# First inverse DFT of a spectral layer as unsplit fp32 products on 32x64 tiles of TensorE, read straight from the second layer's output

## The chip, the core and the metric

One core of a Trainium2 chip runs the whole kernel: TensorE (PE), with its own queue of weight loads (PEld), VectorE (DVE), ScalarE (ACT), GpSimd (POOL), and SyncE (SP), which mostly issues DMAs. The metric is the device time of one execution in microseconds, as the median of several runs; the kernel before takes 1437.01 us (three runs, 1436.25 to 1438.35).

## The reference

The input is 4096 rows of 640 values. It runs through a layer norm, a spectral layer, a residual, a second layer norm and a SwiGLU feed-forward layer (width 1728). The change is inside the spectral layer:

```python
Xf = rfft2(x)                                  # 2049 wave numbers x 640
z  = Xf.reshape(B, H, Wf, NB, BS)              # 4 blocks of 160 columns
h  = relu(complex matmul of z with w1, + b1)   # first layer, per block
o  = complex matmul of h with w2, + b2         # second layer, per block
o  = sign(o) * max(abs(o) - 0.01, 0)           # soft threshold, real and imaginary part
y  = irfft2(o)
```

## The kernel before, in words

**The transforms.** 4096 is 128 x 32, so each DFT is made of two: the forward one of products with 128x128 constants (`dft_a`, then `stage_b`), the inverse one of a first inverse DFT over 32 wave numbers each (`stage_i`) and a second one over 64 complex rows (`first_y` for the first rows, the feed-forward layer's row chains for the rest). The result of the first inverse DFT goes to the DRAM tensor `s2`, from which the second one reads it.

**Chunks and blocks.** The spectrum is cut into 8 chunks `ch` (256 wave numbers each; chunk `CE` = 4 has two more), and each chunk into 4 blocks `b` of 160 columns. A hand-written loop runs over `p = 4*ch + b` from 0 to 31 and writes out the order of the instructions of every engine (`manual_schedule`); `LAST` is 28, and p = 29 to 31 and what follows have code of their own, which I call the tail. In a step p of the loop, TensorE does in this order: the first layer of block p (`stage_l1`, tile `pl`, 21 products of 256 columns), the second forward DFT of a later block (`stage_b`, tile `pb`; two of them where b is 1), the second layer of block p - 1 (`stage_l2`, tile `pc`, 16 products of 320 columns), and the first inverse DFT of row block p - 7 (`stage_i`, tile `pi`).

**From the second layer to the first inverse DFT.** `stage_l2` adds the bias on VectorE and writes the tile `tt` (two per chunk, `q` = 0, 1; 128 wave numbers as rows, real and imaginary parts side by side, 640 columns). A row block i of a chunk needs 64 of these wave numbers, real parts in rows 0 to 63 and imaginary parts in rows 64 to 127; so `move_x` copies them with two DMAs on SP's queue into a tile `xx` (56 DMAs in all). Then ScalarE makes the two halves of the soft threshold (`shrink_parts`), VectorE subtracts them (`shrink`), ScalarE rounds the result to `xh` (`shrink_high`), VectorE takes the rest `xl` (`shrink_low`): operands in the format fp32r are kept as a rounded high part and a low part. `stage_i` makes three fp32r products per half of 320 columns (xh with the constant's high part, xl with it, xh with its low part), six per row block; ScalarE copies each half to a tile `co`, and POOL issues its DMA to `s2`. Chunks 0 to 6 make 28 such row blocks.

**The last chunk** does without the moves: `inverse_last` takes `tt` directly, 64 of its rows at a time, in plain fp32, the real and the imaginary part as two products of 320 columns into the same tile. In the trace each fp32 product stands as two records. Half 0 of its columns runs behind `stage_l2` of the last block, half 1 behind the products `py` of `first_y`, which begin the second inverse DFT of the first four rows. After these come the transposes `pt` and the first products `pg` of the feed-forward layer.

**PSUM.** There are eight banks: tags `p1`, `p2`, `p3` with two each, and `b0`, `b1`. `pl` takes both p1 and, as its third tile, one p3; `pc` takes p2; `pi` takes p3, one bank per half. The third tile of `pl` comes free when ScalarE has copied `u0` out of it and VectorE has made `u1` from it (line 764). A group of products waits for the engine that last read its bank, and what stands behind it in TensorE's queue waits with it.

Of the kernel before, what the change touches and what calls it, by code (L numbers as in the profile page):

```python
# [13 lines left out]
P = 128  # L14
# [32 lines left out]
def constants():  # L47
# [63 lines left out]
    bm = bm.reshape(2, 128, 128)  # L111
    bi = bm[1].reshape(2, 64, 128)

    bx = np.tile(bm[1].reshape(2, 64, 128).transpose(1, 0, 2), (2, 1, 1)).reshape(128, 256)
    bmh, bml = _hl(bm)
    bm = np.stack([bmh, bml], axis=1)
    bm = np.ascontiguousarray(bm.transpose(2, 0, 1, 3)).reshape(128, 2 * 2 * 128)
# [12 lines left out]
    for n in range(4):  # L130
        for h in range(2):
            for r in range(2):
                for i in range(2):
                    m = 4 * (4 * ORDER[-1] + 2 * h + i)
                    ge[64 * i:64 * i + 64, n, 256 * h + 128 * r:256 * h + 128 * r + 128] = (
                        bi[r].reshape(64, 4, 32)[:, :, n] @ ga[n, m:m + 4])
        ge[:, n, 512:] = ga[n]
# [9 lines left out]
        "k_bm": f(bm),  # L147
# [24 lines left out]
def body(tc, x, w1, b1, w2, b2, wg, wu, wd, c, wm, k_fa, k_tb, k_tx, k_bm, k_bx, k_ga, k_ge, k_id, out, dbg=None):  # L172
# [29 lines left out]
    with ExitStack() as top:  # L202
# [34 lines left out]
        with ExitStack() as af:  # L237
# [4 lines left out]
            bm = wp.tile([P, 2, 2, 128], F32R, name="bm")  # L242
# [289 lines left out]
            bx = p2.tile([P, 2, 128], F32, name="bx")  # L532
# [9 lines left out]
            nc.sync.dma_start(bx.rearrange("p a b -> p (a b)"), k_bx)  # L542
# [86 lines left out]
            def stage_b(ch, t):  # L629
                g, tb = gs[ch], tbs[ch]  # L630
                tag = {(0, 1): "p2", (1, 1): "p3"}.get((ch, t))
                pb = (ps.tile([P, 2, 256], F32, tag=tag, name=f"pb{ch}_{t}") if tag else
                      bank0(1 if t == 4 else 0, [P, 2, 256], f"pb{ch}_{t}"))
                col = slice(128 * t, 128 * t + 128)
                for j in range(4):
                    mm(pb[:, :, 64 * j:64 * j + 64], g[:, j, col], tb[:, j, :], start=True, stop=True)
                pbs[ch, t] = pb
# [140 lines left out]
            def stage_l2(ch, b, then=()):  # L778
                h0, h1, r2, _ = hss[ch, b]
                late = []  # L780
                de = slice(160 * b, 160 * b + 160)
                for q in range(3 if ch == CE else 2):
# [3 lines left out]
                    if b == 0 and q < 2:  # L786
                        tts[ch, q] = p2.tile([P, 2, D], F32, tag="tt", bufs=2, name=f"tt{ch}_{q}")
# [13 lines left out]
                    if q < 2:  # L801
                        dve.tensor_tensor(tts[ch, q][:, :, de], pc[:, :320].rearrange("p (r e) -> p r e", r=2),
# [3 lines left out]
                    else:  # L806

                        dve.tensor_tensor(tts[ch, 0][0:1, 1, de], pc[0:1, :160], b2t[0:1, 0, b, :], op=OP.add)
                for q, (pc, seq) in enumerate(late):
                    for i, (l, m) in enumerate(seq):  # L810
                        mm(pc[:, :320], l, m, start=False, stop=(i == 2))
                    dve.tensor_tensor(tts[ch, q][:, :, de], pc[:, :320].rearrange("p (r e) -> p r e", r=2),
                                      b2t[:, :, b, :], op=OP.add)

            xxs = {}

            def move_x(ch, i):
                q, h = i // 2, i % 2
                xx = p2.tile([P, D], F32, tag="xx", bufs=5, name=f"xx{ch}_{i}")
                for r in range(2):  # L820
                    nc.sync.dma_start(xx[64 * r:64 * r + 64, :], tts[ch, q][64 * h:64 * h + 64, r, :])
                xxs[ch, i] = xx


            def shrink_parts(ch, i):
                xx = xxs[ch, i]
                act.activation(cl, xx, AF.Relu, bias=nlam)
                act.activation(xx, xx, AF.Relu, bias=nlam, scale=-1.0)

            def shrink(ch, i):  # L830
                xx = xxs[ch, i]
                if 4 * ch + i < LAST - 5:
                    dve.tensor_tensor(xx, cl, xx, op=OP.subtract)
                else:
                    dve.tensor_scalar(cl, xx, LAM, -LAM, op0=OP.min, op1=OP.max)
                    dve.tensor_tensor(xx, xx, cl, op=OP.subtract)

            def shrink_high(ch, i):
                xx = xxs[ch, i]
                xh = p2.tile([P, D], F32R, tag="xh", bufs=2, name=f"xh{ch}_{i}")  # L840
                xl = p2.tile([P, D], F32R, tag="xl", bufs=2, name=f"xl{ch}_{i}")
                act.activation(xh, xx, AF.Copy)
                xxs[ch, i] = (xh, xl, xx)

            def shrink_low(ch, i):
                xh, xl, xx = xxs[ch, i]
                dve.tensor_tensor(xl, xx, f32(xh), op=OP.subtract)

            def stage_i(ch, i):
                J = 4 * ORDER[ch] + i  # L850
                kd = 0 if J == 0 else 1
                xh, xl, _ = xxs[ch, i]
                co = p2.tile([P, D], F32, tag="co", bufs=2, name=f"co{J}")
                for hf in range(2):
                    e = slice(320 * hf, 320 * hf + 320)
                    pi = (bank0(0, [P, 512], f"pi{J}_{hf}") if ch == NCH - 2 and i % 2 and hf == 0 else
                          ps.tile([P, 512], F32, tag="p3", name=f"pi{J}_{hf}"))
                    mm(pi[:, :320], bm[:, kd, 0, :], xh[:, e], start=True, stop=False)
                    mm(pi[:, :320], bm[:, kd, 0, :], xl[:, e], start=False, stop=False)
# [1705 lines left out]
```

## Time and profile before

| what | value |
|---|---|
| median of three runs | 1437.01 us (1436.25 to 1438.35) |
| profiled execution, first to last instruction | 1434.9 us |
| granted TensorE clock | 1.000 |
| TensorE busy | 1401.5 us (98%) |
| VectorE, ScalarE, POOL busy | 1097.0, 783.8, 538.0 us |
| products of `stage_i` (lines 858 to 860) | 56 of each line, 108.3 to 288.3 us from the start |
| products of `inverse_last` (line 906) | 32 records, 288.7 to 311.1 us |
| `move_x` (line 821) | 56 DMAs of 160 KB |

The spectral layer's loop fills the stretch from about 90 to 262 us, its tail that up to 314 us; the feed-forward layer takes the rest. In the views, `pi<-xh,bm` is a group of instructions that writes tile `pi` from `xh` and `bm`, xN is how many there are, and L858 is a line of the kernel. A record's duration on PE includes the time in which it drains while the next one runs; how long a product holds the engine is seen from start to start.

### The profile page before, as it was taken

The numbers are of one execution on the slowest core, as the hardware profiler recorded it, in microseconds if no ns is written. First come the engines' busy times: TensorE is split into PE (matmuls) and PEld (weight loads), VectorE is DVE, ScalarE is ACT, GpSimd is POOL, SyncE is SP. The second block draws the span as 40 slices with busy tenths as digits, with TensorE's granted clock in tenths as the row PEclk, the third lists the DMA queues.
The fourth block names the chain that finished last, engine by engine and source line by source line (L and its number), as shares of the span: only waits on it lengthen the run. The fifth ranks groups of instructions, "written<-read, shape, count | busy, mean of one in ns | idle before, by whom it ended". The sixth has DMA issues, their size and how long they took to land.

```text
span 1434.9 us, 23925 instructions
## 1 busy us (share of the span) xinstructions
PE 1401.5 (98%) x8516; PEld 1327.5 (93%) x8516; DVE 1097.0 (76%) x1978; ACT 783.8 (55%) x1560; POOL 538.0 (37%) x641
## 2 busy tenths in 40 slices
PE   6899999989999999999999999999999999999999
PEld 2699999968989889899999999999999999999998
DVE  8878888778887687767888778888647768567775
ACT  7868878735545555545555556554435345245432
POOL 5300311154444444323244434434324555146533
PEclk9999999999999999999999999999999999999999
DMA  9988798658677989897887997778796666966652
GB/s 377 322 271 259 242 290 275 218 172 263 232 244 277 339 278 298 323 353 243 279 287 253 343 369 251 253 264 290 280 334 233 208 217 240 359 216 222 207 186 89
DMA packets 187383, 382.28 MB, mean 266 GB/s; under 512 B 22240, under 2 KB 104736, under 8 KB 185472
## 3 DMA queue, kind: packets, MB, share of 16 engines
q1 hardware_dynamic: 179072, 364.37, 74.4%
q0 software_dynamic: 6608, 13.77, 3.0%
q10 hardware_dynamic: 1584, 2.62, 0.5%
q8 instruction: 67, 1.10, 0.3%
q14 instruction: 52, 0.43, 0.1%
HBM read 266.66 MB, written 104.86 MB: 259 GB/s over the span
## 4 chain that ended last, share of the span: by engine, by line
PE 78%; DVE 10%; DMA 7%; ACT 2%; issue 1%; SPq 1%; POOL 1%; DVEq 0%; ACTq 0%; POOLq 0%
PE pd L2435 14%; PE pw L2116 8%; PE pw L2118 8%; PE pw L2117 8%; PE pd_X L2297 5%; PE pc L800 4%; PE pl L732 3%; PE pg L1981 3%; PE pg L1980 3%; PE pg L1982 3%; PE pd_Y L2297 3%; PE pw L2127 2%; PE pw L2129 2%; PE pw L2128 2%; DVE st_a L193 2%; DVE wb L1457 2%
## 5 line engine op out<-in xcount | busy, mean ns | idle before, releaser
L2435 PE MATMUL pd<-wdh,a 128*128 128x320 f32 x1040 | 239.2, 310 | 0.6 <-DVE x L2407 0.6
L2435 PEld LDWEIGHTS pd<-wdh,a 128*128 128x128 f32 x1040 | 176.3, 188 | 1.2 <-DVE x L2407 0.9
L2435 PE MATMUL pd<-wdl,a 128*128 128x320 f32 x540 | 166.2, 309 | 0.0
L1457 DVE TENSOR_TENSOR wb<-r,wb 128x512 fp32r<-128x512 f32 (+3 forms) x154 | 155.9, 1023 | 12.0 <-ACT wb L1454 10.3
L2116 PE MATMUL pw<-h,wt 128*128 128x384 f32 x416 | 141.2, 340 | 2.2 <-ACT s_x L2135 2.2
L2118 PE MATMUL pw<-h,wt 128*128 128x384 f32 x416 | 140.2, 337 | 0.0
L2117 PE MATMUL pw<-h,wt 128*128 128x384 f32 x416 | 139.9, 336 | 0.0
L2407 DVE TENSOR_TENSOR x<-x,pd 128x320 f32<-128x320 f32 x240 | 109.2, 478 | 37.8 <-PE pd L2435 33.4
L1454 ACT ACTIVATE wb<-r 128x512 fp32r<-128x512 f32 (+3 forms) x170 | 117.4, 704 | 34.1 <-PE pw L2129 24.3
L2116 PE MATMUL pw<-h,wb 128*128 128x384 f32 x312 | 104.9, 336 | 0.9 <-DVE x L2407 0.9
L2117 PE MATMUL pw<-h,wb 128*128 128x384 f32 x312 | 104.6, 335 | 0.0
L2118 PE MATMUL pw<-h,wb 128*128 128x384 f32 x312 | 104.6, 335 | 0.0
L1980 PE MATMUL pg<-ht,wb 128*128 128x512 f32 x260 | 102.3, 393 | 0.0
L2435 PEld LDWEIGHTS pd<-wdl,a 128*128 128x128 f32 x540 | 101.4, 188 | 0.3
L1982 PE MATMUL pg<-ht,wb 128*128 128x512 f32 x260 | 101.4, 390 | 0.1
L1981 PE MATMUL pg<-ht,wb 128*128 128x512 f32 x260 | 101.5, 390 | 0.0
L2135 ACT ACTIVATE s_x<-pw 128x384 f32<-128x384 f32 x52 | 25.5, 489 | 121.3 <-PE pw L2118 120.2
L1685 POOL TENSOR_TENSOR cr<-cr,gab 128x640 f32<-128x640 f32 x28 | 47.9, 1712 | 99.3 <-DMA cr<-s 86.5
L2116 PEld LDWEIGHTS pw<-h,wt 128*128 128x128 f32 x416 | 78.1, 188 | 3.6 <-ACT s_x L2135 3.6
L862 POOL DMA_DIRECT2D s<-co x28 | 16.0, 571 | 168.1 <-ACT co L861 159.0
L2117 PEld LDWEIGHTS pw<-h,wt 128*128 128x128 f32 x416 | 78.2, 188 | 0.0
L2118 PEld LDWEIGHTS pw<-h,wt 128*128 128x128 f32 x416 | 78.1, 188 | 0.0
(360 smaller groups left out, 4052.7 us busy)
## 6 DMA issues: line engine op xcount, KB each, us to landing
wt<-td SPq DMA_DIRECT2D x104, 512.0 KB, 5.1
hs<-ho SPq DMA_DIRECT2D x52, 512.0 KB, 5.6
h<-hs SPq DMA_DIRECT2D x32, 768.0 KB, 8.8
r<-in_B_w_up_dram SPq DMA_DIRECT2D x36, 640.0 KB, 4.8
r<-in_B_w_gate_dram SPq DMA_DIRECT2D x36, 640.0 KB, 5.3
wdr<-wdd SPq DMA_DIRECT2D x25, 640.0 KB, 5.7
td<-wt SPq DMA_DIRECT2D x25, 512.0 KB, 6.3
g<-s SPq DMA_DIRECT2D x7, 1280.0 KB, 7.4
```

What stands on the lines that cost most here:

```text
L800: mm(pc[:M, :W], l, m, start=(i == 0), stop=(i == len(seq) - 1))
L1454: act.activation(wbs[t, n][:, 0, ks, e], raw[t, n][:, ks, e], AF.Copy)
L1457: (pool if onp else dve).tensor_tensor(wbs[t, n][:, 1, ks, e], raw[t, n][:, ks, e], f32(wbs[t, n][:, 0, ks, e]), op=OP.subtract)
L1980: mm(b, wh, hh, start=(kk == 0), stop=False)
L1981: mm(b, wh, hl, start=False, stop=False)
L1982: mm(b, wl, hh, start=False, stop=(kk == 4))
L2116: mm(b, w(0, kp), a[:, kp, 0], start=start and kp == 0, stop=False, skip_group_check=not start)
L2117: mm(b, w(0, kp), a[:, kp, 1], start=False, stop=False, skip_group_check=not start)
L2118: mm(b, w(1, kp), a[:, kp, 0], start=False, stop=kp == 1, skip_group_check=not start)
L2297: mm(bk[b, i][:, :320], x, y, start=new and j == 0, stop=j == len(seq) - 1, skip_group_check=not new)
L2407: dve.tensor_tensor(x2[:, e], x2[:, e], x[0][:, :320], op=OP.add)
L2435: mm(pd[g, hf][0][:, :320], l, m, start=i == 0, stop=i == len(s) - 1 and not (last and len(gs) > 1))
```

## The change

- The rows of the spectrum are sorted otherwise: `stage_b` writes its columns in four groups of 32 per parity p in place of two of 64 (the same numbers of columns), so that a tile `tt` with q = p holds the wave numbers of parity p, 32 rows for each row block j.
- `stage_l2` writes half tiles (`tt` for two blocks b, 320 columns; six of them rotate, in place of two whole ones).
- The soft threshold works in place on `tt`. `move_x`, `shrink_high`, `shrink_low`, `xx`, `xh`, `xl` and the constant `bm` are gone.
- `stage_i` now makes the four row blocks of a chunk for half of the columns in one call: 16 fp32 products of 32 rows (contraction) by 64 columns of the constant, 320 columns wide. The row of the tile of TensorE is set by j, its column by q, and each j has a PSUM bank of its own; the two products r = 0, 1 of a tile add up. There are 16 calls; those of chunks 0 to 6 in the loop stand at odd p, **ahead of** `stage_l2`, and take both p1 and both p3 banks. The last chunk uses the same function, and `inverse_last` is gone.
- In the tail VectorE makes the soft threshold alone (`shrink_v`), and the loads of rows of `s2` by SP stand at other places.

```diff
-                    mm(pb[:, :, 64 * j:64 * j + 64], g[:, j, col], tb[:, j, :], start=True, stop=True)
+                    mm(o[:, :, :, j, :], g[:, j, col], tb[:, j, :], start=True, stop=True)
...
-                        tts[ch, q] = p2.tile([P, 2, D], F32, tag="tt", bufs=2, name=f"tt{ch}_{q}")
+                        tts[ch, q, b // 2] = p2.tile([P, 2, 320], F32, tag="tt", bufs=6, name=f"tt{ch}_{q}_{b // 2}")
...
-                for r in range(2):
-                    nc.sync.dma_start(xx[64 * r:64 * r + 64, :], tts[ch, q][64 * h:64 * h + 64, r, :])
...
-                    mm(pi[:, :320], bm[:, kd, 0, :], xh[:, e], start=True, stop=False)
-                    mm(pi[:, :320], bm[:, kd, 0, :], xl[:, e], start=False, stop=False)
-                    mm(pi[:, :320], bm[:, kd, 1, :], xh[:, e], start=False, stop=True)
-                    act.activation(co[:, e], pi[:, :320], AF.Copy)
-                pool.dma_start(s2[4 * J:4 * J + 4].rearrange("k n d -> (k n) d"), co)
+            def stage_i(ch, hf, tag=("p1", "p1", "p3", "p3")):
+                e = slice(320 * hf, 320 * hf + 320)
+                if hf == 0:
+                    cos[ch] = [p2.tile([P, D], F32, tag="co", bufs=4, name=f"co{ch}_{j}") for j in range(4)]
+                co = cos[ch]
...
+                for r in range(2):
+                    for q in range(2):
+                        for j in range(4):
+                            k = slice(32 * j, 32 * j + 32)
+                            kd = 0 if 4 * ORDER[ch] + j + q == 0 else 1
+                            mm(pi[j][64 * q:64 * q + 64, :320], bx[k, kd, r, :], tts[ch, q, hf][k, r, :],
+                               start=(r == 0), stop=(r == 1))
+                for j in range(4):
+                    act.activation(co[j][:, e], pi[j][:, :320], AF.Copy)
...
+                        (pool if hf else nc.scalar).dma_start(s2[m:m + 4, :, e].rearrange("k n d -> (k n) d"), co[j][:, e])
+                    elif hf:
+                        pool.dma_start(s2[m:m + 4].rearrange("k n d -> (k n) d"), co[j])
...
-                on(shrink, p - 6)
+                on(shrink, p - 4)
...
+                inverse(p - 5)
                 on(stage_l2, p - 1)
-                on(stage_i, p - 7)
-                on(shrink_low, p - 6)
-                if p < LAST:
-                    on(shrink_parts, p - 5)
-                if b == 0 and ch:
-                    for i in range(4):
-                        move_x(ch - 1, i)
+                on(shrink_parts, p - 3)
...
+                if p == LAST + 1:
+                    stage_i(NCH - 2, 0)
                 on(stage_l2, p - 1)
-                on(stage_i, p - 6)
-                on(shrink_low, p - 5)
+                if p == LAST + 2:
+                    stage_i(NCH - 2, 1)
+                    load_first_rows(rb, rb + 16, nc.sync)
...
-            for i in range(4):
-                inverse_last(i, 0)
+            stage_i(NCH - 1, 0)
+            stage_l2(NCH - 1, 3, [lambda: shrink_v(NCH - 1, 2), lambda: shrink_v(NCH - 1, 3)])
...
-            for i in range(4):
-                if i == 2:
-                    first_norm(2)
-                inverse_last(i, 1)
+            stage_i(NCH - 1, 1, ("p2", "p1", "p1", "b0"))
+            first_norm(2)
```

**TensorE in the loop.** This is TensorE in step p = 7 (chunk 1, b = 3) of the kernel before; `128x320` is the shape that a product writes, and x3 a run of products with the same operands.

```order
L732 MATMUL pl_3_2_1258<-rz_919,w1c 128x256
L636 MATMUL pb_2_1269<-tb_607,g_605 128x2x64 x4
L800 MATMUL pc_2_0_1282<-w2a,h_2_0_1157 128x320 x3
L800 MATMUL pc_2_0_1282<-w2b,h_2_1_1170 128x320 x3
L800 MATMUL pc_2_0_1282<-w2c,r_1_2_1182 128x320 x2
L800 MATMUL pc_2_1_1292<-w2a,h_2_0_1157 128x320 x3
L800 MATMUL pc_2_1_1292<-w2b,h_2_1_1170 128x320 x3
L800 MATMUL pc_2_1_1292<-w2c,r_1_2_1182 128x320 x2
L858 MATMUL pi_0_1303<-xh_0_1195,bm 128x320
L859 MATMUL pi_0_1303<-xl_0_1196,bm 128x320
L860 MATMUL pi_0_1303<-xh_0_1195,bm 128x320
L858 MATMUL pi_1_1308<-xh_0_1195,bm 128x320
```

The same step of the changed kernel, where `64x320` is one tile's product:

```order
L727 MATMUL pl_3_2_1276<-rz_917,w1c 128x256
L631 MATMUL pb_2_1287<-tb_606,g_604 128x4x32 x4
L837 MATMUL pi_1_0_1297<-tt_0_1_922,bx 64x320
L837 MATMUL pi_1_1_1298<-tt_0_1_922,bx 64x320
L837 MATMUL pi_1_2_1299<-tt_0_1_922,bx 64x320
L837 MATMUL pi_1_3_1300<-tt_0_1_922,bx 64x320
L837 MATMUL pi_1_0_1297<-tt_1_1_933,bx 64x320
L837 MATMUL pi_1_1_1298<-tt_1_1_933,bx 64x320
L837 MATMUL pi_1_2_1299<-tt_1_1_933,bx 64x320
L837 MATMUL pi_1_3_1300<-tt_1_1_933,bx 64x320
```

The inverse products have moved ahead of the second layer; behind these eight (r = 0) stand eight more with the same names (r = 1), and then the six rows of `pc`.

**TensorE in the tail.** The end of the last second layer (`pc_3`) and what follows it, before:

```order
L800 MATMUL pc_3_1_3833<-w2c,r_7_3_3753 128x320 x2
L858 MATMUL pi_0_3846<-xh_3_3801,bm 128x320
L859 MATMUL pi_0_3846<-xl_3_3802,bm 128x320
L860 MATMUL pi_0_3846<-xh_3_3801,bm 128x320
L858 MATMUL pi_1_3851<-xh_3_3801,bm 128x320
L859 MATMUL pi_1_3851<-xl_3_3802,bm 128x320
L860 MATMUL pi_1_3851<-xh_3_3801,bm 128x320
L906 MATMUL pi_0_3860<-tt_0_3595,bx 128x320 x2
L906 MATMUL pi_0_3866<-tt_0_3595,bx 128x320 x2
L906 MATMUL pi_0_3872<-tt_1_3606,bx 128x320 x2
L906 MATMUL pi_0_3878<-tt_1_3606,bx 128x320 x2
L1092 MATMUL py_0_1_3891<-tt_0_3595,et 128x320 x2
```

And in the changed kernel, where the first two rows are the last ones of the call for half 0 of the last chunk:

```order
L837 MATMUL pi_0_2_3720<-tt_1_0_3532,bx 64x320
L837 MATMUL pi_0_3_3721<-tt_1_0_3532,bx 64x320
L795 MATMUL pc_3_0_3746<-w2a,h_3_0_3657 128x320 x3
L795 MATMUL pc_3_0_3746<-w2b,h_3_1_3670 128x320 x3
L795 MATMUL pc_3_0_3746<-w2c,r_7_3_3682 128x320 x2
L795 MATMUL pc_3_1_3758<-w2a,h_3_0_3657 128x320 x3
L795 MATMUL pc_3_1_3758<-w2b,h_3_1_3670 128x320 x3
L795 MATMUL pc_3_1_3758<-w2c,r_7_3_3682 128x320 x2
L1043 MATMUL py_0_1_3778<-tt_0_1_3687,et 128x320 x2
L1043 MATMUL py_0_1_3778<-tt_1_1_3698,et 128x320 x2
L1045 MATMUL py_0_1_3778<-cfrm,et 128x320
L1043 MATMUL py_1_1_3786<-tt_0_1_3687,et 128x320 x2
```

The products of the inverse that stood between `pc_3` and the first `py` now stand ahead of `pc_3`.

**ScalarE at the end of the tail.** The copies of half 1 (`cz`, later `co`), the normalized rows `xn`, and the first steps of the feed-forward layer (`ht`, `hx`), with the engines that each row waits for (DMASW is a DMA that POOL issued, DMAHW one that SP or ACT issued). Before:

```order
L907 ACTIVATE cz_3859<-pi_1_3969 128x320 [waits PE_49]
L907 ACTIVATE cz_3865<-pi_1_3974 128x320 [waits PE_49]
L1118 ACTIVATE xn_2_3979<-x_0_3673,sa_72,ca_71 128x640 [waits DVE_49,Pool_49]
L907 ACTIVATE cz_3871<-pi_1_3981 128x320 [waits PE_49]
L907 ACTIVATE cz_3877<-pi_1_3986 128x320 [waits PE_49]
L1928 ACTIVATE ht_3_4009<-pt_0_4035,sb_74,cb_73 128x512 [waits PE_49]
L1931 ACTIVATE hx_0_4025<-pt_0_4035,sb_74,cb_73 128x512
```

And in the changed kernel:

```order
L1069 ACTIVATE xn_1_3822<-x_0_3586,sa_72,ca_71 128x640 [waits Pool_49]
L840 ACTIVATE co_0_3714<-pi_1_0_3856 128x320 [waits PE_49]
L840 ACTIVATE co_1_3715<-pi_1_1_3857 128x320 [waits PE_49]
L840 ACTIVATE co_2_3716<-pi_1_2_3858 128x320 [waits PE_49]
L840 ACTIVATE co_3_3717<-pi_1_3_3859 128x320 [waits PE_49]
L1069 ACTIVATE xn_2_3884<-x_0_3586,sa_72,ca_71 128x640 [waits DMAHW2_49,DMAHW3_49,DVE_49,Pool_49]
L1877 ACTIVATE ht_3_3904<-pt_0_3930,sb_74,cb_73 128x512 [waits PE_49]
L1880 ACTIVATE hx_0_3920<-pt_0_3930,sb_74,cb_73 128x512 [waits DMAHW6_49,DMASW7_49,DMAHW7_49,DMASW6_49,Activation_49]
```

`xn_2` has moved from between the copies to behind all four, and `hx_0`, which now lies in the memory of `co` tiles, has got waits for DMAs.

136 lines of the change are left out of this document (43 added, 93 removed).

## The prediction

> **What bounds the kernel now.** I read the page first, then the stretches of time, the chain of waits, and single lines.
>
> ```profile
> span 1434.9 us, 23925 instructions
> PE 1401.5 (98%) x8516; PEld 1327.5 (93%) x8516; DVE 1097.0 (76%) x1978; ACT 783.8 (55%) x1560; POOL 538.0 (37%) x641
> ```
>
> The profiled execution spans 1434.9 us; the median of the runs is 1437.0, so 2.1 us lie around the span, and I add them at the end. What this kernel can tell from no change is about 0.2%, 2.9 us. TensorE is the bound of the whole; the table by stretches says how tightly in the two that the change touches, the loop and the tail:
>
> ```profile
> 100.00:256.00 156.00, 154.60 (x1197) 1.00 0.86 265
> 110.00:256.00 146.00, 145.37 (x1131) 144.12 (x1131) 123.93 (x218) 122.68 (x251) 27.69 (x45) 1.00 0.86 269
> 256.00:314.00 58.00, 53.91 (x326) 45.10 (x324) 42.73 (x89) 29.19 (x66) 16.04 (x29) 1.00 0.58 185
> ```
>
> After the lengths stand PE, PEld, DVE, ACT and POOL (PE alone in the first row). In the loop TensorE idles 0.6 us of 146 (1.4 of 156 with the start), so relief for VectorE, ScalarE or SP is worth almost nothing there; only TensorE's own time counts. In the tail it idles 4.1 of 58 us. The chain shows one step of the loop, start and length of each piece:
>
> ```profile
> 242.91 2.52 PE pl L732 x21
> 245.43 0.89 PE pb L636 x8
> 246.32 2.35 PE pc L800 x16
> 248.67 0.14 PE pi L858
> ...
> 249.40 0.15 PE pi L860
> 249.54 2.52 PE pl L732 x21
> ```
>
> So a step is 6.63 us, of which the six products of a row block take 249.54 - 248.67 = 0.87. The tail:
>
> ```profile
> 262.37 0.45 ACT co L861
> ...
> 268.14 5.08 DMA xx<-tt
> ...
> 273.35 0.49 DVE tt L802
> ...
> 284.38 0.42 PE pi L859
> ...
> 288.68 1.31 PE pi L906 x6
> ...
> 290.51 2.22 PE pi L906 x7
> ...
> 293.22 5.06 DMA s<-cz
> 298.41 1.76 DMA cfrm<-s
> 300.22 2.42 PE py L1089 x8
> ...
> 305.33 2.15 PE py L1092 x8
> ...
> 308.03 1.28 PE pi L906 x8
> ...
> 309.83 1.67 PE pi L906 x7
> 311.50 2.07 PE pt L1926 x16
> ```
>
> The moves, then VectorE (273 to 284) and then a trip through DRAM (293 to 300) set this end, and `inverse_last` lies bare twice.
>
> **The price of one new call.** No row shows a 32x64 tile. But `inverse_last` uses tiles of 64 rows, two of them with different rows, so it shows what row tiles do:
>
> ```profile
> L906 PE MATMUL pi<-tt,bx x32: 429/429/533, 288.7 to 311.1; 64*128 64x320 f32 x32
> 307.94:308.00 0.06, 0.04 (x2) 0.04 (x2) 1.00 0.00 0
> ```
>
> Eight fp32 records of 320 columns on all rows take 2.15 us (the piece at 305.33), 0.269 each and 0.537 for a product; eight on two row tiles take 1.28 (at 308.03). The second row, the stretch 307.94 to 308.00 of line 906 alone, shows why: within 0.06 us two products start, of two row blocks. So two row tiles run at once; 4 x 0.269 = 1.08, and the other 0.20 of the 1.28 is the change of tile shape. The longest record, 533 ns against a median of 429, says that half of it is a weight load with nothing to cover it. A new call has 32 records on 8 tiles. If all eight run at once, it holds the engine for 4 x 0.269 = 1.08, and it changes shape twice: 0.37 in all, a little less than 2 x 0.20 since its own loads have 64 columns. **1.45 us a call.** The ends: 1.08 if the change of shape is hidden, 32 x 0.269 = 8.6 if nothing runs at once. I take 1.45, nearest to the row at 308.03. That row tiles run at once is shown; that column tiles do, which share rows, is not. The Trainium skill, TensorE: Matmul & The Clock Gate, Part 3, gives 10.6 times the speed for 16 tiles of 32x32; eight tiles at that yield would make an estimate of 1.6 us for the 16 products, so column tiles run at once there; the sum would be 16 x 0.54 = 8.6 us higher by it, and no run here shows it.
>
> **The loop, up to 256.0.** Line 858 has 56 products for 28 row blocks; the step that starts at 256.0 is p = 28 and does row block 21, so 21 lie before it: 21 x 0.87 = 18.3 us. The changed kernel makes 12 calls up to there (p = 5, 7, ..., 27): 12 x 1.45 = 17.4. **Gain 0.9.** Against that stands a new wait. A call comes ahead of `pc` and takes all four banks of p1 and p3, so its fourth product waits for VectorE to finish `u1` of the same step; before, the 2.35 us of `pc` covered this. Step 249.54 before:
>
> ```profile
> 250.77 0.83 ACT L828 ACTIVATE xx<-xx,nlam 128x640 f32<-128x640 f32 x1
> ...
> 253.08 0.38 ACT L763 ACTIVATE u<-pl 64x256 f32<-64x256 f32 x1
> 253.50 0.47 DVE L764 SCALAR_TENSOR_TENSOR u<-pl,b1r,u 64x256 f32<-64x256 f32 x1
> ```
>
> There `u1` ends 4.4 us into the step, late because ScalarE still makes the threshold of the step before until 2.1 us in. In the changed kernel the step ahead has no copies, so `u0` (0.38) can start when `pl` is done, about 2.7 us in, and `u1` (0.47) ends about 3.7 in. Where b is 3 the call is due at 2.52 + 0.89 = 3.4: 0.3 us of waiting, which delays everything behind it. Where b is 1 a second `pb` (0.89) covers it. VectorE is also at times held up by POOL's work on the down weights:
>
> ```profile
> 215.81 2.38 DVE L556 SCALAR_TENSOR_TENSOR acc<-wm,sc,acc 128x640 f32<-128x640 f32 x1
> 250.35 0.88 DVE L556 SCALAR_TENSOR_TENSOR acc<-wm,sc,acc 128x640 f32<-128x640 f32 x1
> ```
>
> One operation, 2.38 us against 0.88. That falls on two of the b = 3 steps (p = 15, 19): 1 us more each. With 6 x 0.3, 2 x 1.0 less what the lighter VectorE gains, I take **3.0 lost** (0 to 12). At nothing I cost: the columns of `pb` in groups of 32 (same number of columns), the four copies in a row (`pc` behind them covers 2.35), and on queues that have room the removals:
>
> ```profile
> L847 DVE TENSOR_TENSOR xl<-xx,xh 128x640 fp32r<-128x640 f32 x28 | 24.5, 875 | 1.7 <-ACT xh L842 1.7
> L842 ACT ACTIVATE xh<-xx 128x640 fp32r<-128x640 f32 x28 | 20.4, 728 | 4.9 <-DMA xx<-tt 2.5 <-DVE cb L578 1.9 <-ACT we L1032 0.5
> L821 SPq DMA_DIRECT2D xx<-tt x56: 474/594/1654, 93.0 to 268.1; - x56
> ```
>
> 24.5 us of VectorE, 20.4 of ScalarE and 56 issues of SP go, under a TensorE that idles 0.4%. Only the idle 0.8 us of 100 to 110, where the first moves are waited for, comes back: **gain 0.8**.
>
> **The tail, 256 to 314.** Removed from TensorE: seven row blocks, 7 x 0.87 = 6.1; `inverse_last`, 288.68 to 292.73 and 308.03 to 311.50, 7.5; the idle 4.1, of which 0.5 (309.31 to 309.83) lie within those two. Sum 17.2. Added: four calls, 5.8, and six waits. (1) Chunk 6's second call needs the threshold of its last tile, which VectorE makes only after `u1` of p = 30; that ends 0.7 late. (2) The first layer of p = 31 follows at once and needs the first bank copied:
>
> ```profile
> L861 ACT ACTIVATE co<-pi x56: 415/438/441, 110.3 to 288.6; 128x320 f32<-128x320 f32 x56
> L835 DVE TENSOR_SCALAR cl<-xx 128x640 f32<-128x640 f32 x5 | 2.4, 487 | 0.0
> L836 DVE TENSOR_TENSOR xx<-xx,cl 128x640 f32<-128x640 f32 x5 | 4.1, 825 | 0.2
> 310.26 0.92 ACT L1118 ACTIVATE xn<-x,sa,ca 128x640 f32<-128x640 f32 x1 [0.16 <-POOL sa L1112]
> ```
>
> one copy, 0.44, with its start 0.6. (3) Nothing is left between `pc_3` and the first `py` while VectorE makes the last two tiles (0.49 for the bias, 0.49 + 0.83 for the threshold, each): 0.9 and, for the second, 0.6. (4) The rows of `s2` come through DRAM as before, 5.06 + 1.76 and the issues, about 7 us after the last copy, but now under `pc_3` and two `py`: 0.5 is left of the trip. (5) `xn_2` stands behind all four copies, 4 x 0.44 + 0.92 = 2.7 after the call, while `pt` has ten transposes of other rows, 1.3 us at 2.07 for 16: 1.4. (6) `hx_0` waits for the last of POOL's DMAs of `co`:
>
> ```profile
> DMA to landing us min/median/max: 1.8/2.4/5.1
> ```
>
> issued about 2.0 us after the call, it lands 4.4 after it by the median of line 908 and 7.1 by the longest; `hx_0` could start at 2.7 + 1.3 + 0.9 = 4.9, so 0 to 2.2, and I take 0.4. Sum 5.1, so 10.9 added: **gain 6.3**.
>
> **The sum.** 0.9 - 3.0 + 0.8 + 6.3 = 5.0 us less: a span of 1429.9, a time of 1432.0. With the waits from 0 to double, this case reaches from 1427 to 1437.
>
> **The rivals.** (a) *Column tiles overlap only at the seams.* If the records of one row of tiles start in program order, the two records of q = 0 run one after the other, and only the second of them beside the first of q = 1: five times 0.269 a call in place of four, 16 x 0.27 = 4.3 more: 1436.3. For it: an fp32 product is two records on the same tile. Against: the row tiles at 307.94 were not held by that. (b) *Column tiles do not run at once.* Only four tiles do, a call holds 8 x 0.269 = 2.15 + 0.37 = 2.52, 1.07 more: 16 x 1.07 = 17.1, time 1449.1. The gain is gone where a call costs 1.45 + 5.0 / 16 = 1.76 us, and from 1.94 the kernel is slower by more than 2.9. This is the change that does not do what it says; the trace has nothing on it. (c) *The bank wait.* If the fourth product waits for `u1` 1 us in all 12 calls of the loop, 12 in place of 3.0: 1441.0; it is slower by over 2.9 from 0.9 us a call. For it: `u1` 4.4 us into a step before; against: VectorE and ScalarE lose 1.6 us of work per step. (d) *Products start strictly in program order.* Then the second record of a product holds up the next product, and each adds 0.269: 16 x 0.269 + 0.37 = 4.67 a call, 3.22 more, 16 x 3.22 = 51.5: 1483.5. Against it stands the row at 307.94: the first record of the second row block started before the second record of the first one, which stands ahead of it. The Trainium skill states this rule (TensorE: Matmul & The Clock Gate, Part 3: matmuls start and end in program order, only weight loads are pulled ahead); by that row the trace disagrees for row tiles.
>
> **How the numbers follow.** Forecast 0.45, (a) 0.27, (b) 0.14, (c) 0.09, (d) 0.05. Faster by over 2.9 us means below 1434.1: 0.8 of the forecast and a quarter of (a), 0.43. Within: 0.15 of the forecast, half of (a), a little of (c), 0.21. Slower: the rest, 0.36. Time 1432.0; the forecast alone 1427 to 1437; with (a), (c) and half of (b) 1427 to 1449, which leaves out (d), the other half of (b) and the ends, 0.15.
>
> **What would show it.** A call in the loop: from the last `pb` to the first `pc`, 1.45 us (a: 1.72, b: 2.52, d: 4.67), with eight first records started within some 0.1 us. The stretch to p = 28 should end 1.3 later, at 257.3 (17.4 + 3.0 against 18.3 + 0.8), and `pt` should start near 305. A wait of `pi` for line 759 over 6 us in all would make (c) right; a call over 1.76 us makes the forecast wrong, as would a feed-forward layer that changed its length.

## The result and the profile after

The changed kernel takes 1453.26 us (median of 4 runs, 1452.87 to 1454.17), the kernel before beside it 1437.68 (1436.25 to 1440.62): a ratio of 1.0105, 95% interval 1.0091 to 1.0119. It is 16 us slower, where 5 us less was forecast, and outside the range of 1427 to 1449. The page of the changed kernel begins like this:

```profile
span 1451.0 us, 24366 instructions
PE 1403.8 (97%) x8828; PEld 1316.1 (91%) x8828; DVE 1080.9 (74%) x1947; ACT 772.5 (53%) x1538; POOL 536.9 (37%) x640
PEclk9979999999999999999999999999999999999999
```

TensorE is busy for 2.3 us more and the span is 16.1 longer: the loss is almost all waiting. The third character of the clock's row (the slice from 73 to 109 us) is a 7, which the kernel before did not have. So I set the start of the same pieces of work in the two traces side by side. "Third pg" is the third product of the feed-forward layer, the first one that needs a row of `hx`.

| | before | after | later by |
|---|---|---|---|
| first layer of p = 3 starts | 74.9 | 89.8 | 14.9 |
| p = 5 | 89.5 | 105.5 | 16.0 |
| p = 6 | 96.3 | 116.6 | 20.3 |
| p = 28 | 256.0 | 276.3 | 20.3 |
| third pg | 316.0 | 331.3 | 15.3 |
| end of the span | 1434.9 | 1451.0 | 16.1 |

From p = 6 to p = 28, in which nearly all the calls lie, the two kernels need the same 159.7 us. From p = 28 to the third pg the change wins 5.0. The loss lies ahead of p = 6, 20.3 us of it, in a stretch to which the prediction had given a gain of 0.8.

Of the waits of TensorE from 55 to 120 us in the changed kernel these are the longest, with their sum, their number and the longest one:

```profile
PE pc L795 <- DVE tt L807: 10.5, 1, 10.5
PE pc L792 <- POOL w2b L275: 3.0, 1, 3.0
PE pb L631 <- DVE rz L671: 1.1, 1, 1.1
```

The timeline of VectorE says what the 10.5 us were (start, length, and in brackets the idle time ahead of it with what ended it):

```profile
75.02 0.49 DVE L807 TENSOR_TENSOR tt<-pc,b2t 128x320 f32<-128x320 f32 x1 [0.79 <-PE pc L806]
87.00 0.49 DVE L807 TENSOR_TENSOR tt<-pc,b2t 128x320 f32<-128x320 f32 x1 [11.48 <-DMA s<-rst]
```

and that of SP, which issues the DMAs of the first stage:

```profile
79.03 0.59 SPq L348 DMA_DIRECT2D s<-xa  x1
79.66 0.80 SPq L348 DMA_DIRECT2D s<-rst  x1
```

The first write of the first `tt` tile comes at 75.0, that of the second one 12 us later. Its operands (`pc` and the bias) are there; it waits for a DMA that has nothing to do with it, the writing of x rows from the first stage to DRAM. In the kernel before, the same two writes come in one piece, after a wait of 0.57 for `pc`:

```profile
71.88 0.93 DVE L812 TENSOR_TENSOR tt<-pc,b2t 128x320 f32<-128x320 f32 x2 [0.57 <-PE pc L811]
```

What ties the write and the DMA together is memory. The pool of the second layer is opened on the memory that the x tiles of the first stage (`xa0` to `xa7`, 10,240 bytes per partition each) had, and a tile's first write waits for whoever still reads that place. The map of the two programs (bytes per partition):

```
             before              after
xa1          124864-135104       126912-137152
xa2          135104-145344       137152-147392
xa4          155584-165824       157632-167872
xa5          165824-176064       167872-178112
xa6          176064-186304       178112-188352
w2a          124864-135104 xa1   134592-144832 xa1, xa2
w2b          135104-145344 xa2   144832-155072 xa2, xa3
tt, first    155584-160704 xa4   165312-167872 xa4
tt, second   160704-165824 xa4   178112-180672 xa6
```

The change removes `bm` and the tiles of the moves (`xx`, `xh`, `xl`), makes `tt` six small tiles in place of two big ones, and has four `co` tiles in place of two and two places of their own for `xn`. The pool gets 7,680 bytes smaller and lies against the upper end of a region from which `bm` (2,048 bytes) is gone. So the x tiles move up by 2,048, and the weights and the first `tt`, at the lower end of the pool, by 9,728. Of the six places of `tt` the first is the lowest and the second the highest, over `xa6`, which is among the last to be written out. The first of the two rows of SP is the DMA that reads `xa6`: it lands 7.8 us after its issue, at 86.9, and the write of `tt` follows at 87.0. The profile names the second row, which writes the rest of the same rows from `rst`, a tile of another pool; but that one lands at 87.3, when the write had already begun.

That was not the whole price: TensorE's clock fell during the wait. The stretches after the two longest waits, with the granted clock third from the end:

```profile
87.50:92.20 4.70, 4.66 (x20) 4.66 (x21) 3.58 (x8) 0.36 (x1) 0.00 (x0) 0.50 0.89 337
331.30:334.50 3.20, 3.19 (x8) 2.52 (x9) 2.54 (x2) 3.20 (x6) 1.97 (x2) 0.50 0.94 316
```

Half the clock for 4.7 us after a wait of 10.5, and for 3.2 after one of 3.9. The Trainium skill, TensorE: Matmul & The Clock Gate, Part 1, has it so: half rate after an idle window of some 3.4 us, and about as long to come back. The trace agrees for these two waits. After the wait of 3.0 us for `w2b`, which is shorter than that window, the clock was low too: 0.59 from 71.3 to 74.4.

The calls themselves came out better than forecast. In the chain of waits most calls of the loop are like one of these two:

```profile
243.97 1.67 PE pi L837 x32
...
259.33 1.26 PE pi L837 x32
```

and the stretches in which its records start, for line 837 alone (length, busy time and number of the matmul records that are under way in it):

```profile
259.25:259.32 0.07, 0.06 (x8) 0.06 (x9) 1.00 0.01 0
259.57:259.65 0.08, 0.08 (x16) 0.07 (x8) 1.00 2.61 583
259.84:259.92 0.08, 0.08 (x16) 0.07 (x8) 1.00 0.55 190
260.11:260.18 0.07, 0.07 (x16) 0.00 (x0) 1.00 0.88 219
```

Eight records start within 0.07 us, on all eight tiles, and eight more about every 0.27 us: the 32 records go in four rounds (the 16 of the later rows are eight that end and eight that begin). Column tiles do run at once. 4 x 0.27 = 1.08, so the two changes of shape cost 0.18 in all. Three of the twelve calls of the loop are longer: 2.9 us at p = 5 and at p = 17, where `u1` ends late, and 1.9 at p = 9, where VectorE reads one of the banks late for its sums (`pmc`).

At the other end, ScalarE and TensorE where the feed-forward layer begins:

```profile
325.90 0.78 ACT L1877 ACTIVATE ht<-pt,sb,cb 128x512 fp32r<-128x512 f32 x1 [1.27 <-PE pt L1875]
329.17 0.78 ACT L1880 ACTIVATE hx<-pt,sb,cb 128x512 f32<-128x512 f32 x1 [2.49 <-DMA s<-co]
```

```profile
326.73 0.50 PE L1889 MATMUL pg<-ht,wh 128*128 128x512 f32 x1 [0.43 <-ACT ht L1877]
327.07 0.39 PE L1890 MATMUL pg<-ht,wl 128*128 128x512 f32 x1
331.31 0.79 PE L1891 MATMUL pg<-ht,wh 128*128 128x512 f32 x1 [3.85 <-DVE ht L1883]
```

`hx_0` waits 2.5 us for POOL's DMAs of `co`, whose memory it takes, and TensorE 3.85 for the operand made from it, where the kernel before waited 0.9 at the same product:

```profile
316.04 0.50 PE L1942 MATMUL pg<-ht,wh 128*128 128x512 f32 x1 [0.88 <-DVE ht L1934]
```

### The profile page after: what moved, and what is told of

It is laid out like the page before. It is cut to its first block, busy times and chain, and to the rows that moved or that the text cites. A ratio compares the mean times of both kernels' runs of the same rounds, so it can differ in the third digit from the quotient of the medians.

```text
span 1451.0 us, 24366 instructions
## 1 busy us (share of the span) xinstructions
PE 1403.8 (97%) x8828; PEld 1316.1 (91%) x8828; DVE 1080.9 (74%) x1947; ACT 772.5 (53%) x1538; POOL 536.9 (37%) x640
## 4 chain that ended last, share of the span: by engine, by line
PE 83%; DVE 7%; DMA 5%; ACT 3%; issue 1%; POOL 1%; SPq 1%; ACTq 0%; DVEq 0%; POOLq 0%
PE pd L2384 15%; PE pw L2065 8%; PE pw L2067 8%; PE pw L2066 8%; PE pc L795 5%; PE pd_X L2246 5%; PE pl L727 4%; PE pg L1930 4%; PE pg L1929 4%; PE pg L1931 4%; PE pd_Y L2246 2%; PE pw L2076 2%; PE pw L2078 2%; PE pw L2077 2%; PE pb L631 2%; PE py L1651 2%
## 5 line engine op out<-in xcount | busy, mean ns | idle before, releaser
L1406 DVE TENSOR_TENSOR wb<-r,wb 128x512 fp32r<-128x512 f32 (+3 forms) x154 | 152.6, 1001 | 12.2 <-ACT wb L1403 10.8
```

The source lines that it names most:

```text
L1406: (pool if onp else dve).tensor_tensor(wbs[t, n][:, 1, ks, e], raw[t, n][:, ks, e], f32(wbs[t, n][:, 0, ks, e]), op=OP.subtract)
```

## The experiments

The theory (M in the expectations): the change is worth about what was forecast, and 20 us are lost because tiles lie over memory that DMAs still read. The rival (E): the start is late because of the work itself, the first call at p = 5 and what VectorE, ScalarE and SP have to do around it. The ratios are to the kernel before on the same chip (its medians there 1438.1 to 1439.0).

**Move `tt` alone.** Six tags with one place each, which are laid out in rising order:

```diff
-  tts[ch, q, b // 2] = p2.tile([P, 2, 320], F32, tag="tt", bufs=6, name=...)
+  k = (4 * ch + b + q) % 6
+  tts[ch, q, b // 2] = p2.tile([P, 2, 320], F32, tag=f"tt{k}", bufs=1, name=...)
```

> The six tt tiles get six places of their own, in rising order of address; so the second tile lies over xa5 (167872) and no longer over xa6 (178112), which the last DMAs of the first stage still read until 87.0. Theory M (the 20 us of the start are lost because memory is used again too early: the first write of tt waits 11.5 us for those DMAs, TensorE 10.5 us for it, and then runs at half its clock for 4.7 us): pc of p = 2 goes on at about 77 in place of 87.5, 10 to 13 us come back, 1440 to 1443 us; the 3 us of delay that are there before it stay. Rival E (the start is late because the first call at p = 5 and the lists of VectorE and SP around it do not fit): nothing comes back ahead of p = 5, 1450 to 1454 us.

1443.36 us, ratio 1.0032 (1.0020 to 1.0044): 9.9 less than the changed kernel, just short of what M expected. The second write of VectorE:

```profile
75.50 0.49 DVE L808 TENSOR_TENSOR tt<-pc,b2t 128x320 f32<-128x320 f32 x1 [0.79 <-PE pc L807]
78.77 0.49 DVE L808 TENSOR_TENSOR tt<-pc,b2t 128x320 f32<-128x320 f32 x1 [2.78 <-DMA s<-xa]
```

It now lies over `xa5`, and its wait ends when the DMA of `xa5` lands: 2.8 us in place of 11.5. p = 3 begins at 81.6 (89.8). The 3 us of the weights are still there.

**No instruction changed, only an unused tile added.** After the first tiles of `co`:

```diff
+  if ch == 0:
+      p2.tile([P, 1920], F32, name="pad")
```

> No instruction differs from the changed kernel: only a tile of 7,680 bytes per partition that nobody uses is added to the pool of the second layer. It moves the tiles of the pool down by as much, so that w2a, w2b and w2c lie over one tile of x each again, tt over xa4 and xa5, and hx_0 of the feed-forward layer over the unused tile. Theory M: TensorE no longer waits for POOL's w2b (3.0 us), for the second tt at most 2 us (10.5), and hx_0 not for the DMA of co (2.5); 15 and 3 to 4 us come back: 1433 to 1438 us. Rival E: unchanged, 1450 to 1454 us, since every engine has the same list of work.

1442.89 us, ratio 1.0034 (1.0022 to 1.0045): 10.4 less than the changed kernel, little more than half of what I expected. The list of work is the changed kernel's, so E alone cannot explain it. Each wait moved with its address. POOL's first write of `w2a`, first in `e1_ring`, where `w2a` still lies over `xa1` and `xa2`, then here, where it lies over `xa1` alone:

```profile
63.48 3.62 POOL L275 TENSOR_SCALAR w2a<-rm 128x640 fp32r<-128x640 f32 x2 [22.10 <-DMA s<-xa]
```

```profile
59.84 3.62 POOL L275 TENSOR_SCALAR w2a<-rm 128x640 fp32r<-128x640 f32 x2 [18.35 <-DMA rm<-in_A_w_dram]
```

So POOL's `w2b`, which follows it, no longer holds up TensorE (1.2 us for VectorE's part of it is left, as before), and `hx_0`, over the unused tile, follows `ht` at once (at 318.41 after 317.73). But the second `tt` tile came over `xa5` again, and its DMA landed later than I had thought, at 78.7:

```profile
DVE tt L807 <- DMA s<-xa: 6.0, 1, 6.0
```

p = 3 began at 81.5.

**The kernel before, with the same fault put in.** Two unused tiles hold the places of `xx` and `wm` ahead of `tt`:

```diff
+  p2.tile([P, D], F32, tag="xx", bufs=5, name="dx")
+  p2.tile([P, D], F32, tag="wm", bufs=1, name="dw")
```

> The kernel before, with nothing changed but the order of its memory: the places of xx and wm come ahead of tt, so that the second tt tile (176064 to 181184) reaches into xa6, as in the changed kernel. Theory M: its first write waits for the DMAs of the first stage until about 87, and the kernel before loses 11 to 14 us though none of its work changes: 1449 to 1452 us. Rival E: 1437 us.

1452.07 us, ratio 1.0096 (1.0079 to 1.0112): 14.0 us lost by memory alone. The first `tt` tile lies over `xa5` here and the second reaches into `xa6`, and both wait:

```profile
79.48 0.49 DVE L814 TENSOR_TENSOR tt<-pc,b2t 128x320 f32<-128x320 f32 x1 [8.09 <-DMA s<-xa]
87.40 0.49 DVE L814 TENSOR_TENSOR tt<-pc,b2t 128x320 f32<-128x320 f32 x1 [7.42 <-DMA s<-rst]
```

p = 3 began at 90.2. This is nearly as much as the change lost, without the change.

**Both moves of memory.** The edits of `e1_ring` and `e2_pad` together.

> Both moves of memory together: the six tt tiles in places of their own, all over xa4 and the end of it, and the unused tile of 7,680 bytes that puts the weights over one tile of x each and hx_0 over nothing that is still read. Theory M: pc of p = 2 waits for no DMA at all (in e2_pad it still waited 4.0 us, for the write of xa5, and p = 3 began at 81.5 in place of 74.9 in the kernel before), so p = 3 begins at about 75, and 6.5 us come back from 1442.9: 1436 us, a little below the kernel before. Rival E: the loss moves to the next wait of the start, VectorE and ScalarE at p = 4 and 5, and less than 3 us come back: 1440 to 1443 us.

1440.87 us, ratio 1.0018 (1.0009 to 1.0026). p = 3 began at 75.6, as M has it. But p = 3 to p = 6 took 31.1 us (21.4 before), and only 2 us came back: the time of the rival. The cause is still M's. The tile `cl`, into which ScalarE puts the first threshold, had moved over `xa0`, which is written out last of all:

```profile
91.07 0.83 ACT L816 ACTIVATE cl<-tt,nlam 128x640 f32<-128x640 f32 x1 [5.38 <-DMA s<-xa]
```

I had followed the tiles that waited, and not all that moved. In the kernel before `cl` lay there too, but its first use came at 96.97, since the moves delayed the threshold.

**`cl` moved too.** `cl` is made behind `w2c`, over `xa4`; the unused tile has 5,120 bytes:

```diff
-  cl = p2.tile([P, D], F32, name="cl")
   wx = p2.tile([P, P], F32, name="wx")
...
   w2c = p2.tile([P, NB, 640], F32R, name="w2c")
+  cl = p2.tile([P, D], F32, name="cl")
```

> As e3_ring_pad, with cl placed behind w2c, so that it lies over xa4 (done early) and no longer over xa0, whose last DMA is the very last of the first stage (ScalarE waited 5.4 us for it at 85.7 to 91.1 in e3_ring_pad, TensorE 3.2 for ScalarE); the unused tile has 5,120 bytes. Theory M (every loss of the start is a tile that lies over memory still being read): p = 3 to p = 5 takes 15 us in place of 18.0, p = 5 to 6 about 11 in place of 13.2, and 4 to 5 us come back from e3_ring_pad: about 1436 us, 2 to 3 below the kernel before on the same chip. Rival E (the start is bound by its work): less than 1.5 us less than e3_ring_pad.

1436.79 us, ratio 0.9986 (0.9978 to 0.9995): 4.1 less than `e3_ring_pad` and 1.7 less than the kernel before, the first version that beats it. p = 3 to p = 5 takes 14.6 us, as before. Of the waits of the start, all that touch a DMA of the x tiles are gone.

**What is left of E.** p = 5 to p = 6 still takes 11.1 us (6.8 before). Two attempts, the first on `e3_ring_pad`: the thresholds of the first two tiles by VectorE alone, as in the tail.

```diff
-  on(shrink, p - 4)
+  on(shrink_v if p < 6 else shrink, p - 4)
...
-  on(shrink_parts, p - 3)
+  if p > 4:
+      on(shrink_parts, p - 3)
```

> e3_ring_pad, with the thresholds of the first two tiles made by VectorE alone (0.49 and 0.82 us each), as in the tail, in place of ScalarE's two operations (0.82 each) and VectorE's one. In the changed kernel ScalarE makes them at p = 3 and 4 ahead of the rows of z and rz, and TensorE then waits 1.1 us for rz at p = 5 and 1.6 for u1 in the first call. Theory: those waits shrink to 0.3 and 0.5, 1.5 to 2.5 us less than e3_ring_pad: about 1434 us. Rival (VectorE is as late as ScalarE there): same as e3_ring_pad, within 1 us.

1439.41 us, ratio 1.0001 (0.9992 to 1.0010): 1.5 less, but still with the wait for `cl`, on VectorE now. The same edit on `e10_cl`:

> e10_cl with the first two thresholds on VectorE as in e9_ramp. In e9_ramp the wait for cl hid part of what this can bring (p = 5 to 6 still 13.5). Theory: with cl free, rz comes 1 us and u1 1 us earlier at p = 5: 1.5 to 2.5 us less than e10_cl, 1434 us, the fastest of all. Rival (VectorE is as late there): same as e10_cl within 1 us.

1436.20 us, ratio 0.9989 (0.9980 to 0.9998): the same as `e10_cl`. The wait of 1.1 us for `rz` went, and that for `u1` in the first call grew:

```profile
PE pi L840 <- DVE u L759: 1.9, 1, 1.9
```

The second attempt: `e10_cl` with the first call a step later.

```diff
-  inverse(p - 5)
+  if p != 5:
+      inverse(0 if p == 6 else p - 5)
```

> e10_cl with its first call one step later, at p = 6 in place of p = 5, where VectorE has the rows of rz and the second chunk ahead of u1 (the call took 2.9 us there, 1.6 of it waiting for u1). At p = 6 only one pb stands ahead of it, u1 ends some 0.5 us after it, so a call should take 1.26 + 0.5. Theory: p = 5 to p = 7 gets 1 us shorter (16.8 in e10_cl) and the time 1436 us, within what can be told from e10_cl. Rival (what VectorE has to do in the start stays the bound, and the wait moves to p = 6): no change at all between p = 5 and p = 8.

1436.73 us, ratio 0.9990 (0.9980 to 0.9999): no change. p = 5 to p = 6 fell to 8.0 us, but the call took 2.7 at p = 6 too, and p = 8 came 24 us after p = 5, as in `e10_cl`. In `e10_cl`, `e11_best` and `e12_first` p = 8 begins at 115.5, 115.5 and 115.2, though p = 3 begins at 76.5, 75.0 and 76.4. Here E is right: a wait of TensorE that is taken away comes back within a few steps. That VectorE and ScalarE set the pace there is read from the waits; no run takes work off both.

**The call behind the second layer,** where the inverse stood before (on `e3_ring_pad`):

```diff
-  inverse(p - 5)
   on(stage_l2, p - 1)
+  inverse(p - 5)
```

> e3_ring_pad, with the call of the loop behind the second layer, where the inverse stood before. Theory: the wait for u1 goes (0.41 us in six calls, 1.6 in the first), but the first layer of the next step now follows at once and waits 0.5 to 0.6 us for the copy of the first bank, as in the tail at 297.4, in all 12 calls: 6.6 lost and 3.7 won, 2 to 4 us more than e3_ring_pad. Rival (the bank wait on u1 is what the new place of the call costs, as rival c has it): 2 to 4 us less than e3_ring_pad.

1454.29 us, ratio 1.0106 (1.0084 to 1.0127): 13.4 more than `e3_ring_pad`: slower, as expected, but by far more than the 2 to 4 us. TensorE's waits from 110 to 300 us:

```profile
PE pl L727 <- ACT co L843: 6.2, 11, 0.6
PE pl L727 <- DVE tt L804: 5.3, 1, 5.3
PE pi L840 <- DVE tt L804: 1.8, 1, 1.8
```

The first row is the wait that I had priced. The second is one collision: an operation of VectorE stretched beside POOL's.

```profile
218.54 6.95 DVE L820 TENSOR_TENSOR tt<-cl,tt 128x640 f32<-128x640 f32 x1 [4.00 <-ACT tt L817]
```

```profile
218.71 6.09 POOL L592 TENSOR_TENSOR wdf<-wdf,gbb 128x640 f32<-128x640 f32 x4
```

In `e6_late` it is about 0.82 us long elsewhere, but for two more beside such operations of POOL (2.43 and 2.18). Behind the wait TensorE ran at half its clock again (0.51 from 225.7 to 232.6), and this one step (p = 21) lost 7.2 us against `e3_ring_pad`. Without it the call behind the second layer would still be some 7 us slower, an estimate from the start of p = 28, which is 14.5 us later. So the change's place for the call, ahead of the second layer, is the better one.

**Another order of the products** (on `e3_ring_pad`): the four records of a tile one behind the other.

```diff
-  for r in range(2):
+  for j in range(4):
       for q in range(2):
-          for j in range(4):
+          for r in range(2):
```

> e3_ring_pad, with the 16 products of a call in another order: j, then q, then r, so that the two products of a tile, four records, stand one behind the other. If records wait for their own tile alone and those of other tiles go ahead of them, however many stand between, a call stays at 1.26 us and the time that of e3_ring_pad. If TensorE looks ahead only a little or starts in order, each tile but the last holds up the next by three records of 0.27 us: 8 x 0.8 + 0.27 = 6.7 us a call, 5.4 more in 16 calls, 87 us more.

1441.15 us, ratio 1.0016 (1.0006 to 1.0025): the same as `e3_ring_pad`. The calls take 1.31 and 1.66 us. The start of one, for its line alone:

```profile
277.05:277.19 0.14, 0.12 (x8) 0.12 (x13) 1.00 0.52 219
```

Eight records start within 0.1 us although the program has the four records of one tile ahead of the first one of the next. The view does not name the tiles, but a tile takes 0.27 us for each of its records, so the eight are on eight tiles.

**`hx_0` alone** (on the changed kernel): the last four copies and DMAs in another order, since `hx_0` lies over tile 3 of `co`.

```diff
-  for j in range(4):
+  for j in (3, 0, 1, 2) if ch == NCH - 1 and hf else range(4):
```

> The changed kernel, with the four copies and DMAs of the last half taken in the order 3, 0, 1, 2, since hx_0 of the feed-forward layer lies over tile 3 of co. Theory M: hx_0 waits for the first of POOL's four DMAs in place of the last; it starts at about 327.3 in place of 329.2, the second group of pg 1.8 us earlier, and TensorE's time at half clock behind that gap gets shorter: 1.5 to 3 us less, 1450 to 1452 us. Rival (hx_0 waits for something else, or the feed-forward layer makes up for a late start): unchanged, 1453 us.

1455.75 us, ratio 1.0117 (1.0102 to 1.0132): nothing won; `hx_0` waited 2.49 us as before. I had missed 64 bytes: `hx_0` ends at 188416, tile 3 of `co` at 188352, and the rest lies over tile 2, which was now the last one. With the order 2, 3, 0, 1:

> The changed kernel with the last four copies and DMAs in the order 2, 3, 0, 1: hx_0 (186368 to 188416) lies over tile 3 of co and, with its last 64 bytes, over tile 2, which came last in e5_hx. Theory M: hx_0 waits for the second of POOL's DMAs in place of the fourth and starts some 1.2 us earlier after the first pg than in the changed kernel (2.4 us behind it there); 1 to 2 us less. Rival: the gap of 4.2 us between the second and the third product of pg stays, as in e5_hx.

1451.34 us, ratio 1.0092 (1.0079 to 1.0106): 1.9 less than the changed kernel, though the intervals of the two ratios overlap; in the traces the stretch from p = 28 to the third pg takes 53.1 us in place of 55.0. The wait is halved, since `hx_0` now needs the second of the four DMAs and not the last:

```profile
327.81 0.78 ACT L1880 ACTIVATE hx<-pt,sb,cb 128x512 f32<-128x512 f32 x1 [1.23 <-DMA s<-co]
```

## Why the prediction was wrong

**The price of one call** held, and was a little too high: 1.26 us and 1.67 with the wait for `u1`, against 1.45 and 1.75. All eight tiles run at once, so rivals (a), (b) and (d) are out: by the records of the call, and by `e7_order`, which leaves no room for an order in which tiles hold up one another. The two changes of shape cost 0.18 in all; I had taken 0.37 from tiles of 64 rows with 128 columns.

**The loop** held in its sum. From p = 8 to p = 28 (110.0 to 256.0, then 129.9 to 276.3) the changed kernel needs 0.3 us more; the forecast for the loop up to p = 28, without the idle time of the start, was 2.1 more. The twelve calls with their waits take 21.2 us, 2.9 more than the 21 row blocks of the same steps before (18.3), and the first call, which alone takes 2.9, lies ahead of p = 6. That the sum came near is in part luck, since two misses nearly cancel. Each call was priced 0.19 too high. The waits for `u1` come to 5.3 us, and with the others to 6.1, where 3.0 were taken: they are 0.41 us in five of the six calls with b = 3, where 0.3 was taken, but 1.6 each at p = 5 and p = 17, where b is 1 and nothing was. At p = 17 an operation of VectorE took 2.16 us in place of 0.82 beside one of POOL's on the down weights; the prediction had put such collisions at p = 15 and 19. The sign for rival (c) was over 6 us for `u1`, and (c) asked for 1 us in every call, 12 in all: the waits lie between the forecast and (c), and neither holds the loss.

**The ramp** is the step that failed: "Only the idle 0.8 us of 100 to 110, where the first moves are waited for, comes back: gain 0.8". The stretch ahead of p = 6 lost 20.3 us. By their mechanisms:
- about 15 up to p = 3, from memory: 3.1 up to the end of the weights, since `w2a` and `w2b` lay over one x tile more than before (1.5 of it longer waits, 1.3 products at half the clock behind them, and 0.3 were lost ahead of them), 10.5 for the second tile of `tt`, and 1.3 for products at half the clock behind it. `e1_ring`, `e2_pad` and `e4_before_over` show it from both sides, without a change of the work;
- 1.1 from p = 3 to p = 5, the rest of the half clock (p = 3 to p = 5 took 15.7 in place of 14.6, and 14.6 again in `e10_cl`);
- 4.3 from p = 5 to p = 6, which no version wins back (in `e12_first` it only moves to the next two steps): the first call comes there, 2.9 us with its waits, and a wait of 1.1 for `rz`. The changed kernel makes the first threshold two steps earlier, on engines that are late in that stretch. The prediction had the call at p = 5 at the price of any other, and not that VectorE and ScalarE are late there, unlike in the loop.

The words that let this through stand two sentences earlier: "At nothing I cost ...", with a list of operations and issues that go. The diff also took away four kinds of tiles and made six small tiles of two big ones. That is an edit too, to the addresses of every tile behind it, and no term and no rival stood for it; none of the five cases holds the loss.

**The tail** held in its parts and missed one. From p = 28 to the third pg it won 5.0 us; 6.3 was forecast for all of it. Without the wait for `hx_0` it wins 7.8 (52.2 us from p = 28 to the third pg in `e2_pad`, 60.0 before). The term was there, "`hx_0` waits for the last of POOL's DMAs of `co`", with bounds of 0 to 2.2 and 0.4 taken; it measured 2.5 at `hx_0` and 3.0 more than before at TensorE. I had the last landing at 4.4 us after the call, 2.0 for the issue and 2.4 for the DMA. The call ended at 322.3 and the last DMA landed at 329.0, 6.7 after it. The DMA took the 2.4 that I had from the median; the issue was late. The copies were done at 323.8, but POOL's four issues stand behind its part of the row norm, and the last of them came at 326.7:

```profile
324.28 0.55 POOL L1060 TENSOR_TENSOR ca<-ca,mhalf 128x1 f32<-128x1 f32 x1 [0.72 <-DVE ca L1059]
324.86 2.34 POOL L843 DMA_DIRECT2D s<-co  x4
```

The other five waits came to 3.1 us, where 4.7 were summed. The half clock behind the wait for `hx_0` (1.4 us) I had not thought of; the rest of the span is 0.9 longer.

The sum by these steps: 14.9 + 1.1 + 4.3 up to p = 6, 0.0 to p = 28, -5.0 to the third pg, 0.9 behind it: 16.2, against 1451.0 - 1434.9 = 16.1.

With the memory in order the change is worth 1.7 us by the medians (`e10_cl`, ratio 0.9986) and not 5.0. The profiled execution of `e10_cl` (1435.0) shows where the parts are: the tail gives 7.8, p = 5 to p = 6 takes 4.2, the loop 0.5, and 1.6 each are lost ahead of p = 3 and behind the third pg. That sum is 0.1 us more than the kernel before in its own profiled execution (1434.9), so it does not close with the 1.7 less of the timed runs, and single executions scatter by as much. Ahead of p = 3 it is a stretch at half the clock, which `e11_best` does not have; but since p = 8 begins no earlier there, these 1.6 us would not come back. Behind the third pg `e11_best` loses 1.7 as well, at the full clock; what that is stays open.

## What to carry to other kernels

Read the memory map of the two programs before the sum: for every tile whose address moves, ask who read that place last, when that reader is done, and when the tile is first written. An edit that removes or splits buffers can cost more by this than all the work it saves, and the place in the trace is a first write that waits for a DMA of another stage. Repairing one such wait moves other tiles, so look at all that move and at the last bytes of each.

## What the runs showed of the hardware that was not expected

- Eight fp32 products on tiles of 32 rows and 64 columns run fully at once, 32 records in four rounds of 0.27 us, and the order in which they are issued hardly matters (1.26 and 1.31 us a call). The Trainium skill, TensorE: Matmul & The Clock Gate, Part 3, says that matmuls start and end in program order; by `e7_order` the starts of products on different tiles do not. The Trainium skill, TensorEngine Tiling (Array Packing), Key Properties, says that different tiles work independently; the trace agrees.
- A wait of 3.9 us was followed by half the clock during the next 3.2 us (seven products spaced 0.43 in place of 0.23, 1.4 us more), so that wait of TensorE ahead of dense work cost a third more than its length. Its length alone does not decide it: with waits of 1.2 and 0.5 us at the same place, `e10_cl` ran at half the clock from 72.6 to 76.0 and the kernel before at the full one.
- One VectorE operation took 6.95 us in place of 0.82 beside four POOL operations in a row, 6.09 us in all (`e6_late`); in the changed kernel the same operation took 2.16 beside one of them. The prediction had seen 2.38 in place of 0.88 from the same two engines, and had put it at 1 us a time; where TensorE waited for that operation it was 5.
